# Top-k attention beside a SwiGLU FFN: scores ahead of V in the odd turns, the top-k's scratch in the penalty's buffer, transposes behind two FFN pieces

## The chip, the cores and the metric

The kernel runs on one core of one Trainium2 chip. The metric is the device time of one execution in microseconds. Before the change it is 1863.22 us, the median of three runs (1861.03 to 1863.32). All line numbers below are those of the kernel before, unless the text says otherwise.

Engines are named as the profile names them: PE (TensorE, matmuls and transposes), PEld (its weight loads), DVE (VectorE), ACT (ScalarE), POOL (GpSimd) and SP (SyncE, which issues DMAs).

## What is computed

Two blocks, one after the other, in float32. The attention has batch 8, 8 heads, 576 positions and head size 64, and each query keeps only its 32 largest scores. Its output, one row of 512 per token, is the input of a SwiGLU FFN with 4608 tokens and a hidden size of 1536.

```python
scores = scale * np.matmul(q, k.transpose(0, 1, 3, 2))
kth = np.partition(scores, -top_k, axis=-1)[..., -top_k:-top_k + 1]
scores = np.where(scores >= kth, scores, -1000000000.0)
attn = np.exp(scores - np.max(scores, axis=-1, keepdims=True))
attn = attn / (np.sum(attn, axis=-1, keepdims=True) + 1e-09)
x = np.matmul(attn, v)              # then (B,H,S,D) -> (B*S, H*D)
g = x @ w_gate
out = (g / (1 + np.exp(-g)) * (x @ w_val)) @ w_out
```

## The kernel before, in words

**Units and turns.** The attention is cut into 160 units. A unit is one batch, one tile of queries and one pair of heads. 576 positions are four tiles of 128 and a rest of 64, so each batch has four query tiles with 128 rows and one with 64. A unit with 128 rows holds two heads as two stretches of 576 scores; a unit of the rest holds both heads on 128 partitions in one stretch, so it has half the work on DVE (a half unit). The last loop of the kernel runs one turn per unit, and each engine gets its instructions in exactly the order in which this loop writes them: at the end of the kernel every instruction is tied to the one before it on its engine.

**The steps of a unit n, by function and turn.**

- `prep` (L270): PE transposes keys and queries (tile `kqps`), ACT copies them to the slab `kqT` and to `klast`, the block-diagonal of the last 64 keys of both heads. Done once per batch and pair of heads, in turn n - 3 (`fetch`).
- `scores` (L301): written in odd turns, for the two units that follow. PE multiplies the queries by the first 512 keys of each head (tile `s`, L334; half units L326) and by the last 64 keys (tile `last`, L318; half units L328). ACT copies both to `sc` (L337, L340).
- `select` (L344): DVE's top-k. Four rounds of MAX8 (L357), each of which finds eight values of a head; after each of the first three a MATCH_REPLACE8 (L361) overwrites those eight by a very low number in a copy, `rest`. At the end a mask (L367) writes a penalty for every score below the 32nd into `e`.
- `penalize` (L371), in turn n + 1: POOL adds score and penalty in `e` (L379).
- `weigh` (L382), in turn n + 1: ACT takes the exponential of `e` with its row sum (L388).
- `normalize` (L396), in turn n + 2: DVE takes the reciprocal of the sum (L400), ACT scales `e` (L403).
- `turn` (L405), in turn n + 3: PE transposes `e` (tile `etps`, L415), ACT copies it to `et` (L416).
- `values` (L426), in odd turns, for the units n - 5 and n - 4 of that turn: PE multiplies the weights by V (tile `av`, L452; the last keys of both heads by one block-diagonal product, L439). ACT copies the result to `xT` (L467), the FFN's input.

**The FFN.** A block is 256 tokens. Its matmuls are cut into pieces (`feed`, `piece`): four matmuls of the gate or value product (tile `f`, L506), or three of the output product (tiles `y_ps` and `x_ps`, L592), which is written as seven products of a fast scheme with sums on POOL (L578 to L640). A block can start once V of all its tokens is done. ACT's and POOL's parts of a piece are put in the lists `on_act` and `on_pool` and written at the next flush. `share` gives each turn a credit of pieces by a hand-made count, about 6.4 to 7 less the PE work of the attention in that turn.

**An odd turn before.** ACT's leftovers of the FFN, `penalize`, then `values`: the two block-diagonal V products, the `last` scores of the next two units (by `next(nxt)` inside `values`), the other V products, the copies to `xT`. Then the scores of the first unit, their copies, `weigh`, and the copies of the second unit's scores. Then two pieces, the transposes of unit n - 3, and the rest of the pieces between DVE's rounds. **An even turn before** has neither scores nor V and begins with the transposes of unit n - 3.

**Buffers.** PSUM tiles of scores, transposes and V share five banks (`ps_t`); a new tile takes the bank that was freed longest ago in the order of writing. The FFN has three more banks (`ps_f`). `sc` has three buffers, `e` four, `rest` one, `et` two.

Of the kernel before, what the change touches and what calls it, by code (L numbers as in the profile page):

```python
# [11 lines left out]
FP32 = mybir.dt.float32  # L12
# [4 lines left out]
P = 128  # L17
# [11 lines left out]
def kernel(  # L29
# [41 lines left out]
    nc = tc.nc  # L71
# [228 lines left out]

    def scores(ns):  # L301

        scs = [work.tile([P, 2 * S], FP32, tag="sc", name="sc", bufs=3) for _ in ns]
        for n, sc in zip(ns, scs):
            state[n] = dict(sc=sc)

        def bank(name):
            return ps_t.tile([P, 512], FP32, tag="t", name=name)

        qt = units[ns[0]][1]  # L310
        wide = R if qt == J else P
        at = JP if qt == J else S + qt * P
        queries = slice(at, at + wide)
        of = [(preps[units[n][0] * NHP + units[n][2]], units[n][2]) for n in ns]
        last = bank("last")
        for u, (slab, hp) in enumerate(of):
            if qt < J:
                nc.tensor.matmul(  # L318
                    last[:, u * P : (u + 1) * P], slab[:, queries], klast[hp][:]
                )  # L320
        yield
        for u, ((slab, hp), sc) in enumerate(zip(of, scs)):
            if qt == J:
                mains = [bank("s")]
                for d in HALVES:
                    nc.tensor.matmul(mains[0][d, :], slab[d, queries], slab[d, 0:JP])  # L326
                for d in HALVES:
                    nc.tensor.matmul(  # L328
                        last[d, u * P : u * P + R], slab[d, queries], klast[hp][d, d]
                    )  # L330
            else:
                mains = [bank("s") for _ in HALVES]
                for d, ps in zip(HALVES, mains):
                    nc.tensor.matmul(ps[:], slab[d, queries], slab[d, 0:JP])  # L334
            yield
            for hh, ps in enumerate(mains):
                nc.scalar.copy(sc[:, hh * (S + R) : hh * (S + R) + JP], ps[:])  # L337
            if qt < J or u == len(ns) - 1:
                for v in (u,) if qt < J else range(len(ns)):
                    nc.scalar.copy(  # L340
                        scs[v][:, JP : JP + wide], last[:, v * P : v * P + wide]
                    )

    def select(n):  # L344

        nh = n_heads(units[n][1])
        sc = state[n]["sc"]
        m = small.tile([P, 2, TOP_K], FP32, tag="m", name="m", bufs=2)
        heads = [slice(t * S, (t + 1) * S) for t in range(nh)]
        rest = work.tile([P, 2 * S], FP32, tag="rest", name="rest", bufs=1)  # L350
        e = work.tile([P, 2 * S], FP32, tag="e", name="e", bufs=4)
        state[n] |= dict(m=m, e=e, heads=heads)
        cur = sc
        rounds = TOP_K // 8
        for r in range(rounds):
            for t, hs in enumerate(heads):
                nc.vector.max(m[:, t, 8 * r : 8 * r + 8], cur[:, hs])  # L357
# [65 lines left out]

    xT, done = {}, {}

    def values(ns, nxt):  # L426

        b, qt, _ = units[ns[0]]
        last = qt == J
        ql = R if last else P
        ets = [state.pop(n)["et"] for n in ns]
        avs = [ps_t.tile([P, P], FP32, tag="t", name="av") for _ in ns]
        if not last:
            for n, et, av in zip(ns, ets, avs):
                vl = vs[b * NHP + units[n][2]][2]
                nc.tensor.matmul(av[:], vl[:], et[:, J, :], start=True, stop=False)  # L439
        next(nxt, None)  # L440
        for n, et, av in zip(ns, ets, avs):
            hp = units[n][2]
            vt, v_last, _ = vs[b * NHP + hp]
            for c in range(J + 1 if last else J):
                kl = R if c == J else P
                for hh in range(2):
                    moving = (
                        et[0:kl, c, hh * R : (hh + 1) * R]
                        if last
                        else et[:, c + hh * (J + 1), :]  # L450
                    )
                    nc.tensor.matmul(  # L452
                        av[hh * R : (hh + 1) * R, 0:ql],
                        v_last[:, hh, :] if c == J else vt[:, hh, c, :],
                        moving,
                        start=last and c == 0,
                        stop=c == (J if last else J - 1),
                    )
            c0 = b * S + qt * P
            at = c0  # L460
            while at < c0 + ql:
                kb = at // BLK
                n_c = min((kb + 1) * BLK, c0 + ql) - at
                if kb not in xT:
                    xT[kb] = ffn.tile([P, NHP, BLK], FP32, tag="xT", name="xT", bufs=3)
                    done[kb] = 0
                nc.scalar.copy(  # L467
                    xT[kb][:, hp, at - kb * BLK : at - kb * BLK + n_c],
                    av[:, at - c0 : at - c0 + n_c],
                )  # L470
                done[kb] += n_c
                at += n_c
# [232 lines left out]
    def share(n):  # L705


        others = 0.6
        if n % 2 == 1:
            for m in (n - 5, n - 4, n + 1, n + 2):  # L710
                if m >= 0:
                    others += 0.3 if units[m][1] == J else 0.6
        if units[n + 3][1] == 0:
            others += 0.6

        beside = 6.4 if T[1] else 7.0
        return beside * n_heads(units[n][1]) / 2 - others
# [7 lines left out]
        for _ in steps:  # L725
            pass

    def finish_units(ns, nxt):
        values(ns, nxt)
# [5 lines left out]
    load(0)  # L735
    rounding(2)
    load(1)
    load(2)
    run(fetch(0))
    run(scores([0]))  # L740
    run(fetch(1))
# [5 lines left out]
    for n in range(NU + 4):  # L747
        nh = n_heads(units[n][1]) if n < NU else 1
        topk = select(n) if n < NU else no
        over[n - 1] = normalize(n - 1) if 0 <= n - 1 < NU else no  # L750
        if n == 0:
            nxt, ahead = scores([1]), chain(fetch(2), fetch(3))
        else:
            nxt = scores([n + 1, n + 2]) if n % 2 == 1 and n + 2 < NU else no
            ahead = fetch(n + 3) if n + 3 < NU else no
        norm = over.pop(n - 2, no)

        def dve(k, beside=True):
# [48 lines left out]
        dve(1)  # L807
        pieces(1)
        dve(2)
        run(topk)  # L810
        pieces(6)
# [50 lines left out]
```

## Time and profile before

| what | value |
|---|---|
| time, median of 3 | 1863.22 us |
| span of the profiled run | 1860.2 us |
| PE busy | 1703.5 us (92%) |
| PE weight loads busy | 1386.7 us (75%) |
| DVE busy | 1639.4 us (88%) |
| ACT busy | 1198.9 us (64%) |
| POOL busy | 1013.5 us (54%) |
| MAX8, 1152 of them | 614.0 + 205.3 us, 746 to 749 ns each |
| MATCH_REPLACE8, 864 of them | 423.7 + 211.8 us, 742 ns each |
| mask L367, 288 of them | 188.5 us, 691 ns each |
| ACT waiting for V (L467 on L452) | 181.7 us |
| DVE waiting for scores (L357 on L340) | 86.5 us |

The table is from the page of the profile and its list of waits. "Busy" is the time in which an engine executed something; on PE the ends of matmuls are modelled, so that a busy PE need not be at its peak. A line of the waits names the engine and tile that waited, then the one that ended the wait, then the total, the number of waits and the longest. A line of the timeline has start and length in us, engine, line, operation, tiles and count; brackets at its end give the idle time before it and what ended that. One matmul of the program is two entries of the timeline. A wait on an engine that has time to spare costs nothing, so the question for each is whether anything on the way to the end stood behind it.

### The profile page before, as it was taken

How to read it: one execution, taken by the hardware profiler on the slowest of the kernel's cores; microseconds unless marked ns; L12 is line 12 of the kernel's file. 1: busy time of each engine (PE TensorE's matmuls, PEld its weight loads, DVE VectorE, ACT ScalarE, POOL GpSimd, SP SyncE). 2: the span in 40 equal slices, each digit the busy share in tenths (PEclk: the TensorE clock that was granted, in tenths of full speed). 3: DMA queues.
4: the chain of work that ended last, by engine and by line, in shares of the span. 5: the costliest groups of instructions: out<-in, count | busy, mean ns of one | idle time of the engine just before them, and what ended most of it. 6: DMA issues, size and time to landing. Idle time of an engine off the chain costs nothing.

```text
span 1860.2 us, 29955 instructions
## 1 busy us (share of the span) xinstructions
PE 1703.5 (92%) x10500; PEld 1386.7 (75%) x10500; DVE 1639.4 (88%) x3409; ACT 1198.9 (64%) x2847; POOL 1013.5 (54%) x932
## 2 busy tenths in 40 slices
PE   4347899899999999999999999999999999999988
PEld 2236658677787878787788878888788878788877
DVE  6999999999999889999999979998999989999300
ACT  5657766667666676667666676667776767676431
POOL 3556746545464645555465536565446554656534
PEclk7568999999999999999999999999999999999989
DMA  6333130001200020001200011000300011000000
GB/s 171 91 91 91 57 78 14 12 1 29 64 1 12 1 68 25 12 1 27 60 18 1 12 42 50 1 12 2 77 14 12 1 41 40 12 1 13 1 12 12
DMA packets 109142, 59.61 MB, mean 32 GB/s; under 512 B 88512, under 2 KB 96704, under 8 KB 108992
## 3 DMA queue, kind: packets, MB, share of 16 engines
q1 hardware_dynamic: 107936, 57.44, 11.8%
q8 instruction: 83, 1.36, 0.3%
q14 instruction: 67, 0.55, 0.1%
q10 hardware_dynamic: 1056, 0.26, 0.1%
HBM read 48.23 MB, written 9.44 MB: 31 GB/s over the span
## 4 chain that ended last, share of the span: by engine, by line
PE 70%; ACT 10%; POOL 4%; DVE 2%; issue 1%; DMA 0%; POOLq 0%; SPq 0%; ACTq 0%; DVEq 0%
PE f L506 36%; PE x_ps L592 7%; PE av L452 7%; PE etps L415 5%; PE s L334 5%; PE y_ps L592 4%; ACT e L388 2%; ACT et L416 2%; ACT e L403 2%; ACT sc L337 1%; PE s L326 1%; PE last L318 1%; DVE m L357 1%; PE av L439 1%; DVE rest L361 1%; POOL e L379 1%
## 5 line engine op out<-in xcount | busy, mean ns | idle before, releaser
L357 DVE MAX8 m<-rest 128x8 f32<-128x576 f32 x864 | 614.0, 746 | 2.2
L361 DVE MATCH_REPLACE8 rest<-m,rest 128x576 f32<-128x576 f32 x576 | 423.7, 742 | 0.0
L379 POOL TENSOR_TENSOR e<-e,sc 128x1152 f32<-128x1152 f32 (+1 forms) x160 | 382.9, 2393 | 72.5 <-DVE e L367 55.1
L506 PE MATMUL f<-xT,wg 128*128 128x256 f32 x1728 | 404.5, 384 | 0.0
L506 PE MATMUL f<-xT,wv 128*128 128x256 f32 x1728 | 398.9, 382 | 0.0
L506 PEld LDWEIGHTS f<-xT,wg 128*128 128x128 f32 x1728 | 325.8, 192 | 55.3 <-issue 11.1
L506 PEld LDWEIGHTS f<-xT,wv 128*128 128x128 f32 x1728 | 324.5, 191 | 56.8 <-issue 15.2
L534 POOL TENSOR_TENSOR h<-h,half_g 128x512 f32<-128x512 f32 x108 | 140.0, 1296 | 319.4 <-ACT h L533 301.4
L357 DVE MAX8 m<-sc 128x8 f32<-128x576 f32 x288 | 205.3, 749 | 100.5 <-ACT sc L340 86.5
L388 ACT ACTIVATE e<-e,bias 128x576 f32<-128x576 f32 x288 | 223.2, 783 | 97.7 <-POOL e L379 97.1
L415 PE MATMUL etps<-ident,e 128*128 128x128 f32 (+1 forms) x1312 | 190.8, 287 | 71.5 <-ACT sc L337 45.5
L539 POOL TENSOR_TENSOR h<-h,val 128x512 f32<-128x512 f32 x108 | 138.5, 1282 | 193.6 <-ACT val L538 193.1
L415 PEld LDWEIGHTS etps<-ident,e 128*128 128x128 f32 (+1 forms) x1312 | 155.8, 146 | 113.8 <-ACT sc L337 39.5
L403 ACT ACTIVATE e<-e,tot 128x576 f32<-128x576 f32 x288 | 211.5, 787 | 12.3 <-DVE tot L400 12.3
L361 DVE MATCH_REPLACE8 rest<-m,sc 128x576 f32<-128x576 f32 x288 | 211.8, 742 | 0.0
L416 ACT COPY et<-etps 128x512 f32<-128x512 f32 (+1 forms) x448 | 184.8, 490 | 34.8 <-PE etps L415 33.0
L367 DVE TENSOR_SCALAR e<-sc,m 128x576 f32<-128x576 f32 x288 | 188.5, 691 | 3.4
L337 ACT COPY sc<-s 128x512 f32<-128x512 f32 x288 | 154.7, 583 | 54.8 <-PE s L334 44.5
L334 PE MATMUL s<-kqT 64*128 64x512 f32 x512 | 141.5, 652 | 43.5 <-ACT xT L467 36.8
L467 ACT COPY xT<-av 128x128 f32<-128x128 f32 (+1 forms) x192 | 41.3, 241 | 181.8 <-PE av L452 181.7
L452 PE MATMUL av<-et,v 128*64 128x128 f32 (+1 forms) x2560 | 152.2, 271 | 0.0
L531 ACT ACTIVATE h<-f 128x512 f32<-128x512 f32 x108 | 64.5, 597 | 120.5 <-PE f L506 120.5
(76 smaller groups left out, 2137.1 us busy)
## 6 DMA issues: line engine op xcount, KB each, us to landing
v<-in_v_dram SPq DMA_DIRECT2D x32, 256.0 KB, 3.1
kq_in<-in_k_dram SPq DMA_DIRECT2D x63, 128.0 KB, 2.9
kq_in<-in_q_dram SPq DMA_DIRECT2D x63, 128.0 KB, 3.0
w<-in_moe_w_gate_dram SPq DMA_DIRECT2D x12, 512.0 KB, 3.7
w<-in_moe_w_val_dram SPq DMA_DIRECT2D x12, 512.0 KB, 3.7
w<-in_moe_w_out_dram SPq DMA_DIRECT2D x12, 512.0 KB, 3.5
out_dram<-o SPq DMA_DIRECT2D x40, 128.0 KB, 2.4
out_dram<-o SPq DMA_DIRECT2D x16, 256.0 KB, 2.4
```

Of the source, the lines that this page charges most:

```text
L334: nc.tensor.matmul(ps[:], slab[d, queries], slab[d, 0:JP])
L357: nc.vector.max(m[:, t, 8 * r : 8 * r + 8], cur[:, hs])
L361: nc.vector.match_replace(rest[:, hs], m[:, t, 8 * r : 8 * r + 8], cur[:, hs], LOWEST)
L367: nc.vector.tensor_scalar(e[:, hs], sc[:, hs], m[:, t, TOP_K - 1 : TOP_K], FAR, ALU.is_lt, ALU.mult)
L379: nc.gpsimd.tensor_tensor(e[:, every], e[:, every], sc[:, every], ALU.add)
L388: nc.scalar.activation(e[:, hs], e[:, hs], AF.Exp, bias=bias[:, t : t + 1], scale=scale, accum_out=tot[:, t : t + 1],)
L403: nc.scalar.mul(e[:, hs], e[:, hs], tot[:, t : t + 1])
L415: nc.tensor.transpose(ps[0:kl, c * P : (c + 1) * P], e[:, k0 : k0 + kl], ident[:])
L416: nc.scalar.copy(et[0:kl, c0 : c0 + cn, :], ps[0:kl, 0 : cn * P].rearrange("p (c j) -> p c j", c=cn),)
L452: nc.tensor.matmul(av[hh * R : (hh + 1) * R, 0:ql], v_last[:, hh, :] if c == J else vt[:, hh, c, :], moving, start=last and c == 0, stop=c ...
L506: nc.tensor.matmul(ps[:, i, :], w[:, kc, m * P : (m + 1) * P], x[:, kc, :], start=(kc == 0), stop=(kc == KC - 1),)
L592: nc.tensor.matmul(ps, lhsT, T[i][m], start=m == 0, stop=m == MQ - 1)
```

## The change

In an odd turn the scores of the next two units now come ahead of V. `scores` writes the `last` products of both units and the first unit's scores at its first step, that unit's copies and the second unit's scores at its second step, and the second unit's copies at its third. The turn takes the first two steps before anything else, then ACT's leftovers, `penalize`, V and its copies to `xT`, then the third step, and only then `weigh`. In `values` the block-diagonal product closes the sum instead of opening it. For half units the `last` products come before the scores, and each unit's last scores are copied with its own.

The top-k's scratch copy `rest` goes: MATCH_REPLACE8 writes into `e`, which the mask overwrites at the end. `e` gets five buffers for four, since it is now written from the start of a unit's turn.

In even turns the transposes of unit n - 3 come behind two FFN pieces, as they did in odd turns.

`load(2)`, the third load of keys and queries at the start, is issued inside turn 0, just before `load(3)`.

The purpose is that the top-k on DVE gets its scores sooner in a turn, without ACT first waiting for V.

```diff
@@ scores
-        scs = [work.tile([P, 2 * S], FP32, tag="sc", name="sc", bufs=3) for _ in ns]
...
+        first = [bank("s")] if qt == J else [bank("s") for _ in HALVES]
         last = bank("last")
         for u, (slab, hp) in enumerate(of):
             if qt < J:
                 nc.tensor.matmul(
                     last[:, u * P : (u + 1) * P], slab[:, queries], klast[hp][:]
                 )
-        yield
...
+            else:
                 for d in HALVES:
                     nc.tensor.matmul(
                         last[d, u * P : u * P + R], slab[d, queries], klast[hp][d, d]
                     )
+        for u, (slab, hp) in enumerate(of):
+            if u == 0:
+                mains = first
...
+            for hh, d in enumerate(HALVES):
+                ps = mains[0][d, :] if qt == J else mains[hh][:]
+                nc.tensor.matmul(ps, slab[d, queries], slab[d, 0:JP])
             yield
+            sc = work.tile([P, 2 * S], FP32, tag="sc", name="sc", bufs=3)
+            state[ns[u]] = dict(sc=sc)
+            nc.scalar.copy(sc[:, JP : JP + wide], last[:, u * P : u * P + wide])
             for hh, ps in enumerate(mains):
                 nc.scalar.copy(sc[:, hh * (S + R) : hh * (S + R) + JP], ps[:])
@@ select
-        rest = work.tile([P, 2 * S], FP32, tag="rest", name="rest", bufs=1)
-        e = work.tile([P, 2 * S], FP32, tag="e", name="e", bufs=4)
+        e = work.tile([P, 2 * S], FP32, tag="e", name="e", bufs=5)
...
-                        rest[:, hs], m[:, t, 8 * r : 8 * r + 8], cur[:, hs], LOWEST
+                        e[:, hs], m[:, t, 8 * r : 8 * r + 8], cur[:, hs], LOWEST
...
-                cur = rest
+                cur = e
@@ values
-        if not last:
-            for n, et, av in zip(ns, ets, avs):
-                vl = vs[b * NHP + units[n][2]][2]
-                nc.tensor.matmul(av[:], vl[:], et[:, J, :], start=True, stop=False)
-        next(nxt, None)
...
-                        start=last and c == 0,
-                        stop=c == (J if last else J - 1),
+                        start=c == 0,
+                        stop=last and c == J,
...
+        for n, et, av in zip(ns, ets, avs):
+            hp = units[n][2]
+            vl = vs[b * NHP + hp][2]
+            if not last:
+                nc.tensor.matmul(av[:], vl[:], et[:, J, :], start=False, stop=True)
@@ the turn
+        next(nxt, None)
+        next(nxt, None)
         flush(on_act)
         if 0 <= n - 1 < NU:
             penalize(n - 1)
         flush(on_pool)
-        if n % 2 == 0 and n >= TURN:
-            run(turn(n - TURN))
         if n % 2 == 1 and n >= 5:
-            finish_units([n - 5, n - 4], nxt)
-        else:
-            next(nxt, None)
-        for _ in range(2):
-            next(nxt, None)
+            finish_units([n - 5, n - 4])
 
         early[0]()
+        run(nxt)
         if 0 <= n - 1 < NU:
             weigh(n - 1)
-        run(nxt)
 
         dve(2, beside=False)
         if n == 0:
+            load(2)
             load(3)
         if n < NHP:
             load_v(n)
         pieces(2)
         flush(on_act)
-        if n % 2 == 1 and 0 <= n - TURN < NU:
+        if 0 <= n - TURN < NU:
             run(turn(n - TURN))
```

More of the change, by code (lines that the diff above doesn't have):

```diff
@@ L301, in scores @@
     def scores(ns):
-        scs = [work.tile([P, 2 * S], FP32, tag="sc", name="sc", bufs=3) for _ in ns]
-        for n, sc in zip(ns, scs):
-            state[n] = dict(sc=sc)
         def bank(name):
@@ L320, in scores @@
                 )
-        yield
[L322 to L326, printed above, removed]
+            else:
                 for d in HALVES:
@@ L330, in scores @@
                     )
+        for u, (slab, hp) in enumerate(of):
+            if u == 0:
+                mains = first
+            elif qt == J:
+                mains = [bank("s")]
             else:
                 mains = [bank("s") for _ in HALVES]
-                for d, ps in zip(HALVES, mains):
-                    nc.tensor.matmul(ps[:], slab[d, queries], slab[d, 0:JP])
+            for hh, d in enumerate(HALVES):
+                ps = mains[0][d, :] if qt == J else mains[hh][:]
+                nc.tensor.matmul(ps, slab[d, queries], slab[d, 0:JP])
             yield
+            sc = work.tile([P, 2 * S], FP32, tag="sc", name="sc", bufs=3)
+            state[ns[u]] = dict(sc=sc)
+            nc.scalar.copy(sc[:, JP : JP + wide], last[:, u * P : u * P + wide])
             for hh, ps in enumerate(mains):
                 nc.scalar.copy(sc[:, hh * (S + R) : hh * (S + R) + JP], ps[:])
[L338 to L342, printed above, removed]
     def select(n):
@@ L424, with values @@
     xT, done = {}, {}
-    def values(ns, nxt):
+    def values(ns):
         b, qt, _ = units[ns[0]]
@@ L435, in values @@
         avs = [ps_t.tile([P, P], FP32, tag="t", name="av") for _ in ns]
-        if not last:
-            for n, et, av in zip(ns, ets, avs):
-                vl = vs[b * NHP + units[n][2]][2]
-                nc.tensor.matmul(av[:], vl[:], et[:, J, :], start=True, stop=False)
-        next(nxt, None)
         for n, et, av in zip(ns, ets, avs):
-            hp = units[n][2]
-            vt, v_last, _ = vs[b * NHP + hp]
+            vt, v_last, _ = vs[b * NHP + units[n][2]]
             for c in range(J + 1 if last else J):
@@ L726, in run, with finish_units @@
             pass
-    def finish_units(ns, nxt):
-        values(ns, nxt)
+    def finish_units(ns):
+        values(ns)
         for n in ns:
@@ L737 @@
     load(1)
-    load(2)
     run(fetch(0))
```

## The prediction

> **What bounds the kernel now.** I read the page's slices and its chain first (PE carries 70% of the chain), then a table of windows, then the list of waits from 232 us to 1767 us, then the timeline of an odd turn. The windows:
>
> ```profile
> 0.00:186.00 186.00, 97.03 (x460) 68.70 (x462) 170.02 (x360) 113.86 (x251) 96.16 (x92) 0.70 0.40 111
> 186.00:420.00 234.00, 215.54 (x1294) 165.33 (x1291) 226.29 (x472) 159.82 (x382) 135.66 (x114) 0.96 0.11 32
> 420.00:1735.00 1315.00, 1277.72 (x8139) 1055.10 (x8140) 1230.50 (x2553) 885.57 (x2131) 726.88 (x666) 1.00 0.09 23
> 1735.00:1791.00 56.00, 51.30 (x338) 43.69 (x336) 12.57 (x26) 24.22 (x57) 26.12 (x30) 0.94 0.05 10
> 1791.00:1860.20 69.20, 61.90 (x280) 53.85 (x280) 0.00 (x0) 15.46 (x29) 28.69 (x30) 0.94 0.03 8
> ```
>
> Columns: window and length, then busy time of PE, weight load, DVE, ACT, POOL, the granted clock, DMA. Up to 186 us DVE sets the pace (170 of 186 us; PE has no FFN work yet). From 186 to 420 us both are near full. From 420 to 1735 us PE is busy 1277.7 of 1315 us and DVE 1230.5. The last 69.2 us are the last FFN block on PE alone. So the end comes when PE has done its work: the change can gain what PE idles, 37.3 us in the long window and 18.5 in the one before, not what DVE idles. The waits in between:
>
> ```profile
> DVE m L357 <- ACT sc L340: 76.7, 44, 11.8
> ...
> PE kqps L286 <- ACT sc L337: 9.8, 9, 1.3
> PE etps L415 <- ACT e L403: 7.7, 10, 1.4
> PE s L334 <- ACT xT L467: 7.0, 5, 1.7
> PE etps L415 <- ACT sc L337: 6.7, 3, 3.1
> PE x_ps L592 <- POOL h L640: 6.0, 5, 1.7
> PE etps L415 <- issue: 3.6, 5, 0.7
> PE last L318 <- ACT kqT L291: 2.6, 6, 0.5
> ```
>
> DVE waits 76.7 us for scores, the thing that the change goes for; but in stretches with such waits PE is full, as the odd turn at 949.8 us shows:
>
> ```profile
> 949.81 0.50 PE L439 MATMUL av<-et,vlast 128*128 128x128 f32 x3
> 950.15 0.61 PE L318 MATMUL last<-klast,kqT 128*128 128x128 f32 x4
> 950.69 1.97 PE L452 MATMUL av<-et,v 128*64 128x128 f32 x32
> 951.83 0.27 ACT L467 COPY xT<-av 128x128 f32<-128x128 f32 x1 [5.87 <-PE av L452]
> 952.59 1.99 PE L334 MATMUL s<-kqT 64*128 64x512 f32 x8
> 954.70 0.28 ACT L340 COPY sc<-last 128x128 f32<-128x128 f32 x1
> 955.09 1.42 DVE L357 MAX8 m<-sc 128x8 f32<-128x576 f32 x2 [0.21 <-ACT sc L340]
> ```
>
> PE runs V, then scores, with no gap; ACT waits for V before it may copy a score; DVE gets its scores 5.3 us after the turn's start on PE.
>
> **What the Trainium skill says.** "Perfetto Trace Analysis", Identifying the Most-Contended Engine: PE busy time overstates how near PE is to its limit, and weight-load busy time is the better measure. Here that is 1055.1 of 1315 us; still the PE timeline has no gaps in the stretch above, so I take PE as the bound. "TensorE: Matmul & The Clock Gate", Architectural detail: ACT's queue is strictly first in, first out. The trace agrees: the score copies sit behind the xT copy that waited 5.87 us. "Perfetto Trace Analysis", Optimization Strategy: a gap that repeats can mean that buffers ran out. The 1.33 us before a kqps transpose comes at seven of the batch changes and is such a wait for a PSUM bank.
>
> **The change part by part.**
>
> Scores first. Lengths from this turn and the next: a pair of `last` products 0.49 us, four score products 1.91, 16 V products 1.90, a pair of block-diagonal ones 0.49. Before, a score was usable 5.3 us after the turn's start. After: 0.49 + 0.96 for the first unit's two scores + 1.26 for the copies (1.54 from PE's end to DVE's start at 977.07, less 0.28 since the last keys are now copied while scores run) = 2.7 us. DVE's scores come 2.6 us earlier, and V ends at 4.8 us instead of 2.9, 1.9 us later. PE's sum stays. In a stretch where PE is full that moves DVE's idle time and nothing else: 0 us. Where DVE leads the pace, 186 to 420 us, its score waits (2.19, 1.83 and 1.54 us at 259, 326 and 350 us) are on the path: gain up to 5.6, I take 4.
>
> Bank waits. The second unit's scores used the banks of V and waited for xT copies (7.0 us); now V uses the first unit's score banks and waits for their copies. At 765, 1236 and 1618 us ACT was late (held by POOL), for 1.66 us of PE each; there V will wait instead, in the worst case 3 us. I take 0, from -7 to +5.
>
> Second unit's copies ahead of the exponentials. Before, exponentials (some 2 us on ACT) stood between the two units' score copies, and at a batch change a kqps transpose (1.33 us) waited for the bank. That goes, but the even turn's chain of exponentials, et copies and scaling ends about 1 us later. By hand for 1100 to 1111 us: gone 1.33 + 0.65; new 0.5 (`last` is first in the turn and meets kqT being copied), 0.4 (transposes behind V wait for the xT copy) and 0.2. Net -0.9 at seven changes: -6.
>
> Even turn's transposes behind two pieces. Two pieces are 8 matmuls, 1.73 us of PE; the bubbles before those transposes are 0.65 to 0.88 us, `issue` and `e L403` above, 11.3 us in all, of which 4.6 are counted in the line before. Of the other 6.7 I take -4, as ACT's exponentials now stand ahead of the et copies. What queues behind a late et copy is the next turn's V, which has scores in front of it now (2.4 us).
>
> Half turns: `last` products in one run instead of behind each unit's scores. The block took 2.1 us (1068.74 to 1070.84), with 0.29 us weight-load gaps; 16 such turns at 0.1 to 0.2: -2.
>
> FFN behind V. When a block starts right behind V, its first matmul waits for the xT copies (0.2 to see V's end, 0.27 or 0.56 of copies), which the scores used to cover. By the new order six blocks after the first do so: +3.
>
> At no cost: block-diagonal product last (same products); `e` as top-k scratch (same DVE instructions, 742 to 746 ns whatever their tile; with five buffers a unit's predecessor in the buffer was transposed a turn earlier); load(2) later (its scores were copied by 26 us, and DVE starts unit 2 at 42.2). The FFN's due pieces and the last 69.2 us don't change.
>
> Sum: -4 + 0 - 6 - 4 - 2 + 3 = -13 us, some 1851; I say 1852.
>
> **The rivals.** *Most of PE's idle time goes.* DVE, 2.6 us further ahead, frees POOL and ACT of waiting (ACT's exponentials waited 97 us for POOL, POOL 55 us for DVE), and with them PE. For it: nearly all PE waits name ACT or POOL. Against it: the x_ps waits follow the FFN's own chain. 70% of 37.3 plus 4: -30, 1833. *A wash*: the new waits for xT, kqT and banks equal the old ones: 1863. *Slower*: V's delay counts. Where the FFN has run out of work, its next block starts when V is done; if that comes 3 us later at six block starts and the even turns' et copies hold V at a few more (another 1 us at seven batch changes), it is +25, less the -13 that stay: 1875. For it: at 765 us ACT was 2 us late before the change. Against: DVE's greater lead should have POOL's part done earlier.
>
> **How the numbers follow.** Modest gain (1845 to 1858) 0.47, most idle time gone 0.21, wash 0.14, slower 0.18. Likeliest 1852. The range leaves out the far ends of the last two and of the second: 1834 to 1869. Faster 0.67 (the first two, less what lies near the line), same 0.15, slower 0.18.
>
> **What would show it.** Right: DVE's waits for scores fall well below 86.5 us while the time falls by less than 1%; the kqps and s waits are gone from PE's list; new small PE waits `av <- ACT sc`, `f <- ACT xT`; PE idle from 420 us to DVE's end near 30 us. Wrong: PE idle under 15 us (then DVE's lead was worth more than I say), or PE waits for et or score copies of over 20 us (then V's delay is on the path), or a changed mean of DVE's mask (691 ns now, though its median is 512), which I hold constant.

## The result and the profile after

The changed kernel takes 1883.4 us (median of four, 1880.9 to 1888.9), the kernel before 1862.1 us beside it (1859.5 to 1863.3): ratio 1.012, 95% interval 1.0092 to 1.0148. It is 21 us slower. The prediction was 1852, with a range from 1834 to 1869.

What follows reads the changed kernel by its own line numbers: `last` products L315 (half units L320), scores L332, their copies L336 and L338, exponentials L384, transposes L411, et copies L412, V L439, its block-diagonal product L450, copies to `xT` L459.

The same table of windows as before, for the kernel after (window and length, busy time of PE, weight load, DVE, ACT, POOL, granted clock, DMA):

```profile
186.00:420.00 234.00, 216.87 (x1318) 168.21 (x1319) 227.54 (x474) 159.74 (x383) 137.98 (x116) 0.97 0.12 34
420.00:1735.00 1315.00, 1264.22 (x7977) 1040.88 (x7976) 1255.46 (x2537) 867.90 (x2103) 721.35 (x656) 0.98 0.09 23
...
1791.00:1883.90 92.90, 80.17 (x442) 68.98 (x438) 0.33 (x2) 25.46 (x55) 37.63 (x41) 0.95 0.05 12
```

In the long window PE idles 50.8 us where it idled 37.3, and its clock is 0.98 where it was 1.00. Both show in the number of PE's entries there: 7977 for 8139. The rest is done after 1735 us. From 186 to 420 us next to nothing was won: PE idles 17.1 us there for 18.5.

The list of waits of the kernel after, PE alone, 420 to 1735 us (total, number, longest):

```profile
PE s L332 <- ACT et L412: 13.4, 5, 2.8
PE last L315 <- ACT kqT L291: 6.9, 6, 1.8
PE kqps L286 <- ACT et L412: 6.7, 7, 1.2
PE kqps L277 <- DMA kq_last<-in_q_dram: 6.0, 6, 1.4
PE kqps L286 <- DMA kq_in<-in_k_dram: 5.6, 7, 1.8
PE x_ps L584 <- POOL h L632: 5.2, 5, 2.9
```

The waits that the change was to take away are gone (scores for `xT` copies, and most of `kqps` for score copies), but larger ones stand in their place. By what ended them, PE's idle time in this stretch was 23.4 us on ACT, 8.9 on POOL, 2.1 on DMAs and 2.9 of `issue`; now it is 33.0 on ACT, 12.5 on DMAs and 5.2 on POOL. So the waits for loads of keys and queries grew as much as those for ACT.

DVE did get its scores. In the list of waits from 232 to 1767 us its wait for them, 76.7 us before, is now, in the kernel after,

```profile
DVE m L353 <- ACT sc L338: 30.2, 16, 11.7
```

and the time rose all the same. Part of this wait only moved: DVE's waits for POOL's read of `m` and for ACT's `tot` grew there from 10.8 to 39.8 us. One of the five waits of `s`, in the timeline of the kernel after (start and length in us):

```profile
1239.41 2.52 POOL L632 TENSOR_TENSOR h<-h,xT 128x256 f32<-128x256 f32 x3
...
1242.07 2.62 POOL L375 TENSOR_TENSOR e<-e,sc 128x1152 f32<-128x1152 f32 x1
...
1243.29 0.61 PE L315 MATMUL last<-klast,kqT 128*128 128x128 f32 x4
...
1243.83 1.12 PE L332 MATMUL s<-kqT 64*128 64x512 f32 x2
...
1244.73 0.77 ACT L384 ACTIVATE e<-e,bias 128x576 f32<-128x576 f32 x1 [8.13 <-POOL e L375]
...
1246.85 1.24 ACT L412 COPY et<-etps 128x512 f32<-128x512 f32 x3
...
1247.48 3.78 PE L332 MATMUL s<-kqT 64*128 64x512 f32 x6 [2.54 <-ACT et L412]
```

POOL comes to the penalty only after its sums for the FFN. ACT stands 8.1 us before the exponentials, and the et copies queue behind them. The next turn's scores, now first on PE, need the banks that those copies empty. And the six entries of `s` after the wait take 3.78 us, where eight took 1.99 in the kernel before: the clock is at half. The windows around it, kernel after (same columns):

```profile
1240.00:1244.00 4.00, 4.00 (x21) 3.47 (x21) 2.52 (x5) 0.00 (x0) 4.00 (x5) 1.00 0.01 4
1244.00:1248.00 4.00, 1.46 (x4) 0.64 (x6) 4.00 (x11) 3.24 (x10) 1.68 (x4) 0.81 0.01 2
1248.00:1252.00 4.00, 4.00 (x14) 1.62 (x13) 4.00 (x9) 3.04 (x7) 3.35 (x2) 0.50 0.00 0
```

PE counts as busy from 1248 to 1252 us, but with 14 entries, where the first window has 21. So slow work passes as busy time: from 186 us on PE's grew by 10.8 us for nearly the same number of entries (10064 for 10051). I added up (1 - granted clock) times length from end to end; with the idle time it gives, for 420 to 1735 us:

| kernel | PE idle | lost to half clock |
|---|---|---|
| before | 37.3 us | 1.7 us |
| after | 50.8 us | 22.2 us |
| scores first alone (below) | 48.1 us | 8.5 us |
| copies ahead alone (below) | 40.2 us | 6.8 us |
| even turns behind two pieces alone (below) | 49.2 us | 13.7 us |

From before to after that is 13.5 + 20.5 = 34 us. In the other two stretches after 186 us idle time and lost clock together fall by 4.8 us. The other 5.5 us between this and the 23.7 us of the two spans are PE work done faster or counted twice (idle time inside a half-clock stretch); that I did not separate.

One more row, the mask of the kernel after (busy, mean ns, idle before): DVE's busy time rose by 35 us and all of it is here, 811 ns in place of 691.

```profile
L363 DVE TENSOR_SCALAR e<-sc,m 128x576 f32<-128x576 f32 x288 | 223.4, 811 | 1.1
```

The Trainium skill, "SBUF — State Buffer", SBUF: two separate sides, says that DVE and POOL share a pair of ports under an exclusive lock, and that an operation such as TENSOR_SCALAR, in the mode that uses both of DVE's port pairs, holds it for its whole length. The trace of the kernel after agrees: the 117 masks during which POOL ran nothing take 0.49 to 0.52 us, the longest beside a POOL sum 2.9 us. In the kernel before 158 masks met no work of POOL.

### The profile page after: what moved, and what is told of

It is laid out like the page before. It is cut to its first block, busy times and chain, and to the rows that moved or that the text cites. A ratio compares the mean times of both kernels' runs of the same rounds, so it can differ in the third digit from the quotient of the medians.

```text
span 1883.9 us, 29895 instructions
## 1 busy us (share of the span) xinstructions
PE 1721.2 (91%) x10500; PEld 1397.3 (74%) x10500; DVE 1674.6 (89%) x3409; ACT 1193.5 (63%) x2847; POOL 1020.7 (54%) x932
## 4 chain that ended last, share of the span: by engine, by line
PE 67%; ACT 11%; POOL 7%; SPq 1%; DMA 1%; issue 1%; DVE 1%; POOLq 0%; ACTq 0%
PE f L498 36%; PE av L439 7%; PE s L332 7%; PE x_ps L584 5%; PE etps L411 5%; PE y_ps L584 3%; ACT e L384 3%; POOL e L375 2%; ACT et L412 2%; PE av L450 2%; ACT e L399 2%; POOL p L570 2%; PE last L315 1%; POOL h L632 1%; ACT sc L338 1%
## 5 line engine op out<-in xcount | busy, mean ns | idle before, releaser
L353 DVE MAX8 m<-e 128x8 f32<-128x576 f32 x864 | 612.6, 743 | 2.2
L357 DVE MATCH_REPLACE8 e<-m,e 128x576 f32<-128x576 f32 x576 | 422.8, 739 | 0.0
L498 PE MATMUL f<-xT,wg 128*128 128x256 f32 x1728 | 396.8, 381 | 0.0
L384 ACT ACTIVATE e<-e,bias 128x576 f32<-128x576 f32 x288 | 224.1, 789 | 132.6 <-POOL e L375 132.5
L332 PE MATMUL s<-kqT 64*128 64x512 f32 (+1 forms) x640 | 193.5, 678 | 48.4 <-ACT et L412 41.8
L363 DVE TENSOR_SCALAR e<-sc,m 128x576 f32<-128x576 f32 x288 | 223.4, 811 | 1.1
L411 PE MATMUL etps<-ident,e 128*128 128x128 f32 (+1 forms) x1312 | 179.8, 282 | 44.4 <-ACT e L399 21.1
L357 DVE MATCH_REPLACE8 e<-m,sc 128x576 f32<-128x576 f32 x288 | 211.3, 739 | 0.0
L411 PEld LDWEIGHTS etps<-ident,e 128*128 128x128 f32 (+1 forms) x1312 | 156.8, 145 | 67.4 <-issue 31.8
L439 PEld LDWEIGHTS av<-et,v 128*64 128x64 f32 x2560 | 143.5, 149 | 81.4 <-ACT sc L338 62.0
L412 ACT COPY et<-etps 128x512 f32<-128x512 f32 (+1 forms) x448 | 181.8, 480 | 14.1 <-PE etps L411 14.1
L338 ACT COPY sc<-s 128x512 f32<-128x512 f32 x288 | 159.1, 607 | 49.8 <-PE s L332 49.8
L439 PE MATMUL av<-et,v 128*64 128x128 f32 (+1 forms) x2560 | 164.5, 284 | 12.2 <-ACT sc L338 8.3
L336 ACT COPY sc<-last 128x128 f32<-128x128 f32 (+1 forms) x160 | 42.2, 264 | 193.5 <-PE last L315 161.7
```

Source lines behind the costliest of these rows:

```text
L332: nc.tensor.matmul(ps, slab[d, queries], slab[d, 0:JP])
L357: nc.vector.match_replace(e[:, hs], m[:, t, 8 * r : 8 * r + 8], cur[:, hs], LOWEST)
L363: nc.vector.tensor_scalar(e[:, hs], sc[:, hs], m[:, t, TOP_K - 1 : TOP_K], FAR, ALU.is_lt, ALU.mult)
L384: nc.scalar.activation(e[:, hs], e[:, hs], AF.Exp, bias=bias[:, t : t + 1], scale=scale, accum_out=tot[:, t : t + 1],)
L411: nc.tensor.transpose(ps[0:kl, c * P : (c + 1) * P], e[:, k0 : k0 + kl], ident[:])
L412: nc.scalar.copy(et[0:kl, c0 : c0 + cn, :], ps[0:kl, 0 : cn * P].rearrange("p (c j) -> p c j", c=cn),)
```

## The experiments

Each ratio is to the kernel before on the same chip.

### First group: which part, and is DVE's growth the loss?

My first theory, T1, took the turn above for the whole story: even turns' et copies sit behind exponentials. T2 blamed V's new place, T3 the scratch in `e`.

**Even turns' transposes first again** (after):

```diff
+        if n % 2 == 0 and n >= TURN:
+            run(turn(n - TURN))
         if n % 2 == 1 and n >= 5:
             finish_units([n - 5, n - 4])
...
-        if 0 <= n - TURN < NU:
+        if n % 2 == 1 and 0 <= n - TURN < NU:
```

> The kernel after, but in even turns the transposes of e stand ahead of the two FFN pieces again, as in the kernel before; all else as after. T1 (the even turn's et copies now come behind that turn's exponentials on ACT, which wait for POOL's penalty, and the next odd turn's scores, first on PE, wait for the banks that those copies must empty; PE then stands some 2.5 us and the clock halves after it): 1855 us, between 1845 and 1865; the waits of s for et copies (57.5 + 41.8 us in after) nearly gone. T2 (V behind the scores delays the FFN's blocks): 1875 or more, the waits of s for et copies may go but the time stays. T3 (the top-k's scratch in the penalty's buffer slows DVE's mask, 811 ns for 691): 1875 or more, mask still near 800 ns.

Measured: 1889.2 us, ratio 1.0154 (1.0136 to 1.0173), no faster than after and by the medians 6 us slower (the intervals overlap). The waits of scores for et copies are gone, but its list of PE waits (420 to 1735 us) begins with

```profile
PE etps L411 <- ACT e L399: 12.1, 8, 1.7
PE av L439 <- ACT sc L338: 9.8, 3, 3.4
```

T1 as a whole story fell: the wait moved to V, which now needs banks that score copies free, and to the transposes.

**Even turns' transposes behind two pieces, alone** (before):

```diff
-        if n % 2 == 0 and n >= TURN:
-            run(turn(n - TURN))
...
-        if n % 2 == 1 and 0 <= n - TURN < NU:
+        if 0 <= n - TURN < NU:
```

> The kernel before, with only one part of the change: in even turns the transposes of e stand behind two FFN pieces. T1 says that this part does the harm where it meets an odd turn that starts on PE with work needing those copies; here that turn starts with V, which needs the et tiles themselves: slower than before, 1870 to 1885 us, with waits of av for et copies. T2 and T3, which put the loss elsewhere: 1862 us, within 4.

Measured: 1875.9 us, 1.0074 (1.0057 to 1.0092). As T1 said: the wait is of V for et copies, in the place of `etps` waits:

```profile
PE av L439 <- ACT et L416: 19.5, 5, 3.9
```

T1 had not named a second cost of this part: PE's waits for the loads of keys and queries, 2.1 us before, are 9.6 us here, 12.5 in after, and at most 0.9 in the three runs with even turns' transposes first (first run above, copies ahead and scores first below). The tile of such a load has one buffer, so the load is issued only once the keys before it have been transposed, and behind other loads in SyncE's queue. At 907 us in after, those transposes end at 902.9 us, a load of V occupies the queue until 903.0 us, the loads of keys and queries are issued from 903.1 to 906.4 us, and PE waits for two of them, which land at 907.3 and 908.8 us. That PE's earlier waits, ahead of the keys, covered this in the kernel before would fit, but no run tests it.

**Scratch in `e`, alone** (before):

```diff
-        rest = work.tile([P, 2 * S], FP32, tag="rest", name="rest", bufs=1)
-        e = work.tile([P, 2 * S], FP32, tag="e", name="e", bufs=4)
+        e = work.tile([P, 2 * S], FP32, tag="e", name="e", bufs=5)
...
-                        rest[:, hs], m[:, t, 8 * r : 8 * r + 8], cur[:, hs], LOWEST
+                        e[:, hs], m[:, t, 8 * r : 8 * r + 8], cur[:, hs], LOWEST
```

> The kernel before, with only one part of the change: the top-k's scratch is the penalty's buffer e, with five buffers, and no rest. T1 and T2: 1862 us, within 3, mask at 691 ns. T3: slower, 1868 to 1885 us, with the mask at 780 ns or more.

Measured: 1862.9 us, 1.0009 (1.0000 to 1.0017), mask at 688 ns. T3 is out: this part costs next to nothing. The mask is longer in every run with scores first (812 ns in scores first alone), where more masks fall beside POOL's work.

**Exponentials behind the et copies in even turns** (after):

```diff
-        if 0 <= n - 1 < NU:
+        if n % 2 == 1 and 0 <= n - 1 < NU:
             weigh(n - 1)
...
         if 0 <= n - TURN < NU:
             run(turn(n - TURN))
+        if n % 2 == 0 and 0 <= n - 1 < NU:
+            weigh(n - 1)
```

> The kernel after, with PE's order unchanged, but in even turns the exponentials of unit n - 1 stand behind the transposes of unit n - 3, so that on ACT the et copies come ahead of the exponentials that wait for POOL. T1 (it is the exponentials ahead of the et copies on ACT that hold the banks): 1858 us, between 1848 and 1868, the waits of s for et copies nearly gone. T2 and T3: 1880 or more.

Measured: 1878.3 us, 1.0079 (1.0052 to 1.0107). The scores wait for et copies no more, but at three of the five places V waits 2.9 us for score copies: some 5 us come back, not 25, and the interval reaches into that of after.

### Second group: which engine is the bound?

In before, after and the first run above the span is the end of DVE's last mask plus 103.0 us, to 0.1 us. That suggested T4: DVE's order of work sets the end, and its 35 us more are the loss. The prediction had said the opposite.

**MAX8 over 544 of 576 scores**, in after and in before, which leaves 32 keys out of the search:

```diff
-                nc.vector.max(m[:, t, 8 * r : 8 * r + 8], cur[:, hs])
+                few = slice(t * S, t * S + S - 32)
+                nc.vector.max(m[:, t, 8 * r : 8 * r + 8], cur[:, few])
```

> The kernel after, with MAX8 over 544 of each head's 576 scores, which leaves 32 keys out of the search: 1152 MAX8 by some 33 ns, DVE does 38 us less, nothing else changes. T4 (it is DVE's own order of work that sets the end: its last top-k and then a fixed 103 us; so the 35 us by which the mask grew are the loss): 1845 us, between 1838 and 1860. T1 (PE is the bound and its waits for banks and copies are the loss): 1878 or more.

> The kernel before, with MAX8 over 544 of each head's 576 scores, which leaves 32 keys out of the search: DVE does 38 us less. T4: the kernel before too follows DVE, 1830 us, between 1822 and 1845. T1 and the prediction's step that PE is the bound from 186 us on: 1858 or more, with DVE's waits for scores grown by over 30 us.

Measured: after so cut, 1889.4 us, 1.0136 (1.0111 to 1.0161); before so cut, 1860.3 us, 0.9986 (0.9976 to 0.9995). MAX8 takes 38 us less in both, but the masks grew by 14 us in after and by 17 in before, so DVE's busy time fell by 23 and 21 us. That gives nothing in one and 2.6 us (0.9 to 4.5) in the other, where DVE's waits for scores grew from 86.5 to 105.0 us. T4 is out.

**No block-diagonal V product** (after), which leaves the last 64 keys of full units out of the sum:

```diff
-                        stop=last and c == J,
+                        stop=c == (J if last else J - 1),
...
-            vl = vs[b * NHP + hp][2]
-            if not last:
-                nc.tensor.matmul(av[:], vl[:], et[:, J, :], start=False, stop=True)
```

> The kernel after without the block-diagonal V product of the last 64 keys of each full unit (left out of the computation): PE does 128 products less, some 31 us, DVE's work stays. T1: 1855 us, between 1848 and 1863. T4: 1878 us, between 1872 and 1886.

Measured: 1847.6 us, 0.9913 (0.9893 to 0.9933). Against after, that is 36 us less, and PE's busy time is 33 us less (1687.9 for 1721.2); the rest is shorter waits. PE is the bound.

**Four buffers for `m`** (after):

```diff
-        m = small.tile([P, 2, TOP_K], FP32, tag="m", name="m", bufs=2)
+        m = small.tile([P, 2, 16], FP32, tag="m", name="m", bufs=4)
...
```

The lines left out let rounds two to four write their eights to the same place.

> The kernel after, with four buffers for the eights that MAX8 finds, m, for two (a tile keeps only the first eight and the latest eight, so it is half as large): DVE's 29.7 us of waits for POOL's read of m go. T4: 1862 us, between 1853 and 1872. T1: 1883, within 4.

Measured: 1888.1 us, 1.0151 (1.0117 to 1.0184), no faster than after. DVE's waits for POOL's read of `m` (29.7 us over the whole run) are gone, but those for `tot` grew from 45.2 to 67.1 us, so most of this wait moved.

### Third group: the parts of the order, and the clock

T5: PE is the bound, and the loss is its new gaps with the half clock after them. T6: the half clock has another cause or costs nothing. T7: the second unit's copies ahead of the exponentials do all the harm.

**Second unit's copies ahead of the exponentials, alone** (before), and **scores first without the other two parts** (after, with both undone):

```diff
+        run(nxt)
         if 0 <= n - 1 < NU:
             weigh(n - 1)
-        run(nxt)
```

> The kernel before, with one part of the change: in odd turns the copies of the second unit's scores stand ahead of the exponentials on ACT. T5 (PE is the bound; its new gaps, some 13 us, and the half clock after them, some 16 us, are the loss, and this part is harmless, as the prediction has it, -6 at the batch changes): 1856 us, between 1850 and 1861, the kqps waits for score copies gone. T7 (this part is what makes the exponentials and with them the et copies and the next turn's copies late): 1868 or more.

> The kernel after with even turns' transposes first and the exponentials ahead of the second unit's copies again, both as in the kernel before: what is left is scores ahead of V (with the top-k's scratch in e, which costs nothing). T5 (V's banks now wait for score copies, which sit behind exponentials on ACT): slower than before still, 1880 to 1897, with waits av <- ACT sc of 3 us at the three places near 770, 1250 and 1640 us. T7: 1862 to 1870.

Measured: copies ahead 1868.4 us, 1.0036 (1.0020 to 1.0052); scores first 1881.8 us, 1.0105 (1.0087 to 1.0122). So T7 is out, though its forecast for the first of the two came, and T5's rider that the copies are harmless is out too: each part costs by itself. For scores first, idle time and lost clock from 186 us on grew by 18.4 us and the span by 18.2. In the first the `kqps` waits for score copies fell from 8.5 to 1.6 us, and its list shows where they went (the first of these rows was 5.6 us in before, the second 0.6):

```profile
PE etps L415 <- ACT e L403: 12.2, 8, 1.7
...
PE kqps L286 <- ACT et L416: 4.9, 6, 1.0
```

The scaling of e on ACT follows the exponentials, so it comes later by what was put ahead of them. In scores first, the list begins with

```profile
PE av L439 <- ACT sc L338: 9.6, 3, 3.3
```

three waits of V for score copies in place of three waits of scores for `xT` copies (5.0 us).

**Needless PE work in the gaps** (after):

```diff
+        if ns[0] in (64, 72, 108, 144, 152):
+            for _ in range(6):
+                nc.tensor.matmul(last[:, 2 * P :], klast[of[0][1]][:], of[0][0][:, 0 : 2 * P])
         for u, (slab, hp) in enumerate(of):
             if u == 0:
                 mains = first
```

> The kernel after, with six needless products of 256 columns (some 2.3 us) between the last-keys products and the scores in the five odd turns (63, 71, 107, 143, 151) in which PE stands 2.5 to 2.8 us before its scores: they fill these gaps and write to a part of the bank that nobody reads. T5 (the gap makes the clock drop): the clock stays at full speed after these five places, which cost 13.6 us of clock in after: 1871 us, between 1866 and 1877. T6 (the drops don't come from these gaps, or cost nothing): 1883 or a little more.

Measured: 1897.5 us, 1.0188 (1.0161 to 1.0214). It does not answer its question: I had counted the turns wrongly, and the products stood four turns early, where PE had no gap. It weighs PE work once more: 13.8 us of busy time in those products, and the kernel is 14 us slower than after.

**Exponentials behind copies and pieces in all turns** (before):

```diff
-        if 0 <= n - 1 < NU:
-            weigh(n - 1)
         run(nxt)
...
             run(turn(n - TURN))
+        if 0 <= n - 1 < NU:
+            weigh(n - 1)
```

> The kernel before, with the exponentials moved on ACT behind the second unit's copies, the FFN's parts of two pieces and, in odd turns, the et copies: ACT no longer stands before POOL's penalty with copies behind it that PE needs. T5: the kqps waits for score copies (8.5 us) and the s waits for xT copies (5.0 us) go and nothing else grows on PE: 1850 us, between 1845 and 1857. T7: 1868 or more.

Measured: 1927.0 us, 1.0348 (1.0320 to 1.0376), the worst of all, and a plain miss. The `kqps` waits did go, but its list of PE waits from 420 to 1735 us now begins with transposes that wait for e, 35 times:

```profile
PE etps L415 <- ACT e L403: 49.2, 35, 2.7
```

**The fillers in the right turns** (after): 68, 76, 112, 148, 156 for `ns[0]`, three products.

> The kernel after with three needless products of 256 columns (0.76 us each, 2.3 us together) between the last-keys products and the scores, now in turns 67, 75, 111, 147 and 155, the five in which PE stands 2.5 to 2.8 us before its scores (the earlier fillers stood four turns too early). T5 (a PE gap of this length is what halves the clock after it): the five gaps shrink to under 0.6 us, the clock stays full after them, and of the 13.6 us of clock lost there some 10 come back: 1872 us, between 1866 and 1877. T6 (the drops have another cause, or cost nothing): 1883 or more, with the gaps filled and the clock still at half after these places.

Measured: 1879.1 us, 1.0079 (1.0048 to 1.0110): with 7.5 us of needless work the kernel is 4 us faster than after. A product takes 0.5 us, not the 0.76 that I had reckoned, so the gaps shrank to 1.2 to 1.5 us and not to 0.6, and the time lies outside T5's 1866 to 1877. The place shown above, in this kernel, timeline and windows:

```profile
1238.53 1.46 PE L325 MATMUL last<-kqT,klast 128*128 128x256 f32 x6
...
1239.92 1.12 PE L335 MATMUL s<-kqT 64*128 64x512 f32 x2
...
1242.30 1.98 PE L335 MATMUL s<-kqT 64*128 64x512 f32 x6 [1.26 <-ACT et L415]
```

```profile
1236.00:1240.00 4.00, 4.00 (x22) 3.31 (x20) 3.05 (x7) 0.46 (x1) 3.51 (x4) 1.00 0.01 2
1240.00:1244.00 4.00, 2.74 (x8) 1.05 (x8) 4.00 (x11) 3.97 (x11) 2.16 (x3) 1.00 0.00 0
1244.00:1248.00 4.00, 3.35 (x40) 2.85 (x40) 4.00 (x8) 2.50 (x11) 2.62 (x2) 1.00 0.00 0
```

The clock stays at 1.00 and six entries of `s` take 1.98 us for 3.78. At four of the five places it stays full; at all five together 13.7 us of lost clock became 1.7, though other places lost more than in after. The sum over the spans from 186 us on: lost clock -4.4, idle -6.9, needless work +7.5, together -3.8, where the two spans differ by 6.5 and the medians by 4.3. The mechanism of T5 is shown; of its amount, 13.7 us at five places, only a part came back. The interval of this ratio reaches into that of after, so the time alone doesn't settle it; the clock at the five places does.

### Fourth group: can a gap of the kernel before be filled?

**One FFN piece ahead of the keys' transposes** (before), in turns 17, 37, ... and then in turns 19, 39, ...:

```diff
         flush(on_pool)
+        if n % 20 == 17:
+            credit[0] -= piece()
         next(ahead, None)
```

> The kernel before, with one FFN piece ahead of the keys' transposes in the one turn of each batch change in which they wait 1.33 us for a bank (turns 17, 37, 57 and so on), taken from the next turns' credit. If PE is the bound and its gaps are what can be gained, the kqps waits for score copies (8.5 us in all) shrink to 3 or less: 1856 us, between 1851 and 1861. If the gap only moves to the next wait on PE, as with the second unit's copies ahead of the exponentials: 1861 or more.

> The kernel before, with one FFN piece ahead of the keys' transposes in turns 19, 39, 59 and so on, where PE waits 1.33 us for a bank until the second unit's score copies are done (the earlier piece stood two turns before this wait). If such a gap can be filled with work that has to be done anyway: the kqps waits for score copies fall from 8.5 us to 2 or less and the time by 4 to 8 us: 1856 us, ratio 0.9955 to 0.998. If the gap moves to the next wait on PE: 1861 or more, ratio above 0.999.

Measured: 1864.8 us, 1.0013 (1.0004 to 1.0022) with 17, where the piece stood two turns before the wait and left it as it was; 1858.0 us, 0.9978 (0.9969 to 0.9987) with 19. There the `kqps` waits for score copies fell to 0.5 us and PE idles 33.9 us between 420 and 1735 us, for 37.3 in before. So a gap can be filled with work that is due anyway; it moves when something else on ACT is put off for it.

**Needless products in the two waits before the last V** (before), and both together:

```diff
+    def needless(k):
+        ps = ps_f.tile([P, 2, BLK], FP32, tag="f", name="fill")
+        for _ in range(k):
+            nc.tensor.matmul(ps[:, 0, :], ident[:], wg[:, 0, 0:BLK])
...
+        if n == NU + 2:
+            needless(1)
         if n % 2 == 0 and n >= TURN:
...
+        if n == NU + 1:
+            needless(4)
         if n % 2 == 1 and 0 <= n - TURN < NU:
```

> The kernel before, with needless products (0.76 us each) only where PE waits anyway: four in the 3.2 us before the transposes of unit 158, one in the 1.3 us before those of unit 159, at 1781 to 1787 us. In the kernel before the clock is at half from about 1785 to 1793 us after this wait, under the last V products and the first products of the last FFN block. T5 (a PE gap halves the clock, and the half clock is paid in full): the clock stays full, 1859 us against 1862.4, 3 to 4 us less, ratio between 0.9975 and 0.9990. T6 (the drops have another cause, or cost nothing): 1862 to 1863.5, ratio 1.000 or more.

> The kernel before with both the piece ahead of the keys' transposes in turns 19, 39 and so on, and the needless products in the two waits near 1785 us. If both gains hold and add: 1853 us, ratio 0.994 to 0.997. If only the filled end holds: 1860 us, ratio 0.9985 to 0.9995.

Measured: 1859.5 us, 0.9988 (0.9981 to 0.9995), and together 1852.8 us, 0.9953 (0.9940 to 0.9965). The first in windows, the kernel before and then with the products:

```profile
1784.00:1788.00 4.00, 2.15 (x9) 1.69 (x10) 0.04 (x1) 2.13 (x6) 0.00 (x0) 0.58 0.19 45
1788.00:1792.00 4.00, 4.00 (x45) 3.06 (x44) 0.00 (x0) 1.16 (x4) 0.00 (x0) 0.50 0.00 0
```

```profile
1784.00:1788.00 4.00, 2.83 (x30) 2.14 (x28) 0.16 (x1) 1.75 (x5) 2.18 (x3) 1.00 0.50 114
1788.00:1792.00 4.00, 2.91 (x36) 2.18 (x38) 0.00 (x0) 2.46 (x9) 0.00 (x0) 1.00 0.10 21
```

Work that computes nothing makes the kernel faster by 1 to 3.5 us, because it lies in a wait and keeps the clock up. With the piece it is the fastest kernel of the study that leaves nothing out of the computation: 9 us below before, 31 below after.

## Why the prediction was wrong

Two steps failed. The prediction let the new waits on PE come out no larger than those that go (bank waits: "I take 0"; the copies ahead: "Net -0.9"), and it priced each wait by its length alone. Between 420 and 1735 us PE idles 13.5 us more, and the half clock takes another 20.5. The three parts, in the order in which the runs add them up to the change:

| part | predicted | measured by the ratios |
|---|---|---|
| scores first (with half turns, FFN behind V) | -4 + 0 - 2 + 3 = -3 us | +20 us |
| second unit's copies ahead of the exponentials | -6 us | +9 us on top (+7 alone) |
| even turns' transposes behind two pieces | -4 us | -6 us on top (+14 alone) |

The values on top are differences of two ratios, good to about 5 or 6 us, so that the -6 is hardly clear of nothing.

*PE is the bound, DVE's waits for scores are worth nothing.* Right. 21 to 23 us less on DVE gave 0 to 2.6, 33 us less on PE gave 36, and 46.5 us less of score waits came with a longer time. Two of the signs of being wrong came. The mean of the mask changed, by 35 us in all, but DVE's work is not what the time follows. PE's waits for et and score copies passed 20 us in after (13.4 + 6.7 in the list above, and 1.8 more), but it was scores and the keys' transposes that waited, not V.

*Scores first: gain where DVE leads, 4.* Wrong: from 186 to 420 us PE idles 17.1 us for 18.5, and 19.5 in scores first alone.

*Bank waits: "there V will wait instead, in the worst case 3 us. I take 0".* The place and the mechanism were right and the worst case came: 3.1 to 3.3 us at three places, 9.6 us for 5.0. With `last` waiting for kqT (6.0 for 2.6) and smaller ones PE's idle time grew by 10.8 us.

*Copies ahead: "Net -0.9 at seven changes".* This step failed by its sign. I had seen that the chain of exponentials, scaling and et copies ends later, but let only transposes behind V pay for it. The transposes that wait for e itself pay: -6.9 us on `kqps` for score copies, +6.6 on `etps` for e and +4.3 on `kqps` for et copies.

*Even turns: "What queues behind a late et copy is the next turn's V, which has scores in front of it now".* The scores in front need banks too and wait themselves, five times for 2.5 to 2.8 us. The 9.6 us of waits for the loads of keys and queries are not in the prediction at all. That the amount on top comes near the -4 is luck: behind the other two parts this one also took away the transposes' waits (12.1 + 2.9 us) and three waits of V (9.8 us), and alone it costs 14 us.

*The term that is not in the sum at all* is the clock. I reckoned every wait at its own length. Before, a wait of 1.66 us usually cost 1.66 us; after, many are beyond what the clock bears, and the half clock after them costs more than the waits: 20.5 us against 13.5 between 420 and 1735 us. Scores first alone has 6.8 us of it. The rival "slower", at 1875, had the sign and the et copies; of V's delay at the FFN's block starts only 1.3 us was to be seen, in scores first alone.

## What to carry to other kernels

Where PE is the bound, each wait that an edit moves must be followed to the instruction that now stands there, and to everything queued behind it on the engine that releases it: here each part removed the wait that it aimed at, and longer ones came in its place, from the same ACT queue and, with the even turns' part, from loads into a single buffer. Price a PE gap by its length plus the half clock that may follow it (the next section says when), and look at the granted clock in windows of a few us, since PE's busy time counts slow work as work. A small gap is best filled with work due anyway, and one that can't be closed may be worth filling with needless products.

## What the runs showed of the hardware

The clock falls after much shorter waits than I had in mind. The Trainium skill, "TensorE: Matmul & The Clock Gate", What's actually happening, speaks of half rate after an idle window of some 3.4 us. In the long stretch (420 to 1735 us) of the two kernels and the seventeen experiments, 42 of 50 PE gaps of 2 to 4 us have a stretch of low clock between 4 us before and 8 us after them, and even 58 of 232 gaps of 1.2 to 2 us. The size agrees with the page: the losses come as 1.7 or 3.4 us, which is half of one or two windows of 3.4 us. Why one gap is followed by it and the next isn't, the traces of the 19 kernels tell. The granted clock changes only at whole multiples of 3.41 us. Cut into these windows from 186 us to the end, there are 138 at full clock in which PE was busy for less than 45%, and each of them is followed by one at half clock. Of the 8697 with more than 65% none is, and of the 254 in between 55 are. So here a window need not be idle throughout, as the page has it: what decides is PE's idle share of one window, not the length of a gap. The wait of `s` at 762.7 us in the kernel after, 2.75 us long, lies almost whole in the first of two such windows (same columns):

```profile
761.78:765.19 3.41, 0.94 (x2) 0.11 (x1) 3.41 (x9) 2.55 (x7) 0.85 (x2) 1.00 0.00 0
765.19:768.60 3.41, 3.13 (x6) 1.33 (x6) 3.41 (x9) 3.41 (x9) 3.31 (x3) 0.50 0.01 2
```

The wait of 1.66 us at 1234.4 us in the kernel before is spread over two windows, which keep 2.69 and 2.48 us of busy time, and the clock stays full.

A kernel's last DVE mask can keep a fixed distance to its end (103.0 us in three kernels) without DVE being the bound: only taking work away told which engine led.
